# mLSTM cell and SwiGLU layer: another order of the opening, with smaller first weight pieces

## The chip, the cores and the metric

The kernel runs on one core of a Trainium2 chip. Times are device microseconds of one execution. The times before are from three runs; the profile is of one further execution.

## The reference

Two layers are computed one behind the other, all values float32 (the weights are float64 in memory and are rounded to float32 by the kernel).

```python
B, H, S, D = 4, 8, 768, 40                     # q, k, v, o_gate: (B, H, S, D)
for t in range(S):                             # first layer: an mLSTM cell, per head
    m_new = maximum(f[t] + m, i[t])
    fs, is_ = exp(f[t] + m - m_new), exp(i[t] - m_new)
    C = fs * C + is_ * outer(v[t], k[t])
    n = fs * n + is_ * k[t]
    y[t] = sigmoid(o[t]) * (C @ q[t]) / maximum(abs(n @ q[t]), 1)
x = y as (B*S, H*D) = (3072, 320)
g = x @ w_gate                                 # second layer: 320 -> 1536
out = (g * sigmoid(g) * (x @ w_val)) @ w_out   # 1536 -> 320
```

## The kernel before

**Tiling.** The sequence of 768 steps is cut into six chunks of 128. The cell is computed chunk by chunk in its parallel form: within a chunk the recurrence becomes a masked product of q and k, weighted, times v, and only a state passes between chunks. For each chunk the feed-forward layer is run on the 4*128 tokens of the four batch entries. The 1536 hidden features are twelve blocks of 128. `hidden(g, m)` (L646) makes hidden block m of chunk g with ten pairs of products (L651), then Silu on ScalarE (L656) and a product on VectorE (L657). `project` and `project_all` multiply the twelve hidden blocks by `w_out`. While the feed-forward layer of one chunk runs on TensorE, the cell of the next one is worked in between its blocks; lists called `slots` and `after` say behind which block.

**The opening.** Before the first hidden block there is the cell of chunk 0, with a code of its own. Its four units are the four batch entries, with eight heads each; units 0 and 1 form half P=0, units 2 and 3 half P=1. In words: q and k are transposed on TensorE (`first_turn`), their products taken (`first_scores`) and weighted on VectorE (L523), multiplied by v (`first_own(u)`, L530), divided (`first_x(u)`, L535 to L538) and gated by the sigmoid of o_gate (`sig`, L463; `first_gate(P)`, L544). `first_gate` then has GpSimd copy 64 columns (L545). `first_seam(P)` transposes the result into `xT` on TensorE and copies it out of PSUM on ScalarE and VectorE; `first_state(P)` makes the state for the next chunk. `burn(n)` is n products of constants whose result nobody reads. `turn_one` and `turn` are the later chunks' way of transposing q and k: 16 transposes of 64 rows in place of 8 of 128 rows.

**The weights.** Each weight block arrives as pairs of 32-bit words. `piece_load(p)` (L140) asks for piece p of the list `PIECES` (L138): `gv` pieces hold one or two blocks of `w_gate` (lower 64 partitions) and `w_val` (upper 64), `o` pieces four blocks of `w_out`. The gate half is issued from SP; the value half from ScalarE for p < 5, and from SP otherwise. A piece lies in one of two `raw` buffers, or in a `home`: a stretch of `h_sb` or `wo_sb` that is not yet or no longer in use. `W0`, the weights of the first cell, is the first eight blocks of `h_sb`, so a home in there waits for the products that read them. A block is then converted to float32 in three steps: `scale` (two ScalarE instructions, L190 and L192, into `top`, of which there is one buffer, and `low`), `join` (two on VectorE, L199 and L200) and `rounded` (L207, on VectorE or GpSimd).

**What sets the order.** The kernel is under `tc.manual_schedule()`: each engine executes its instructions in the order in which the code writes them, and waits are set from the data. DMAs are instructions of the queue that issues them (SP, or ScalarE between its other work). A DMA takes one of eight semaphores in turn, and so waits for the DMA eight before it to have landed.

Of the kernel before, what the change touches and what calls it, by code (L numbers as in the profile page):

```python
# [12 lines left out]
U32 = mybir.dt.uint32  # L13
AF = mybir.ActivationFunctionType
ALU = mybir.AluOpType
# [9 lines left out]
def kernel(  # L25
# [112 lines left out]
    PIECES = [("gv", 0, 1), ("gv", 1, 1)] + [("gv", m, 2) for m in range(2, NFC, 2)] + [("o", m, 4) for m in range(0, NFC, 4)]  # L138

    def piece_load(p, home=None):  # L140
        kind, m, n = PIECES[p]
        if kind == "gv":
# [3 lines left out]
            queues = (nc.sync, nc.scalar if p < 5 else nc.sync)  # L146
# [12 lines left out]
        if home is None:  # L159
            raw = conv.tile([128, 4 * NKC * 128], U32, name="raw")  # L160
        else:
            raw = home.rearrange("p a t -> p (a t)").bitcast(U32)
# [22 lines left out]
    def scale(j):  # L185
        if j in blocks:
# [3 lines left out]
            nc.scalar.mul(top, hi.bitcast(F32), 2.0 ** -112)  # L190
            low = conv.tile([128, NKC * 128], I32, name="low").rearrange("p (a d) -> p a d", a=a)
            nc.scalar.mul(low, lo, 2.0 ** -29)  # L192
            blocks[j] = (low, top.bitcast(U32), dst)
# [97 lines left out]
    def turn_one(P, src, dst, engs):  # L291
        tp = [bank("tp_kq").rearrange("p (a t) -> p a t", t=SUB) for _ in range(2)]
# [181 lines left out]
    A, V, G = nc.scalar, nc.vector, nc.gpsimd  # L474
    HH = H // 2
# [65 lines left out]
    def first_gate(P):  # L541
        for u in (2 * P, 2 * P + 1):
            x = x_sb[:, u, 0:DM].rearrange("p (h d) -> p h d", d=D)
            nc.vector.tensor_tensor(x, x, o_sb[:, u * H:(u + 1) * H], op=ALU.mult)  # L544
# [13 lines left out]
    def first_seam(P, engs):  # L558
        for c, eng in zip(range(0, NKC, 2), engs):
# [5 lines left out]
            copy(eng, xT(0)[:, c:c + len(cs), 2 * P * L:(2 * P + 2) * L].rearrange("p c (u s) -> p c u s", u=2), tp)  # L565

# [13 lines left out]
    first_turn(1, k_sb, kT, (A, A))  # L580
    first_x(0)
    first_turn(1, q_sb, qT, (A, V))
    load(o_sb, o_gate, 0, 1)
    piece_load(0)
# [5 lines left out]
    piece_load(1)  # L590
    burn(3)
    first_own(2)
    piece_load(2, h_sb[:, 1:1 + NKC])
    sig(1)
    burn(2)
    first_own(3)
    first_gate(0)
    first_x(2)
    first_x(3)
    first_gate(1)  # L600
    first_seam(0, (A, A, V))
    scale(0)
    ps1 = first_state(1, "gen")
    burn(1, "gen")
    piece_load(3, h_sb[:, NH - NKC:])
    join(0)
    first_seam(1, (A, A, V))
    rounded(0, V)
    first_kept(0, first_state(0), A)
    first_kept(1, ps1, V)  # L610
    convert(1, V)
    nc.scalar.activation(warm, warm, AF.Silu)
    piece_load(4, wo_sb)
    piece_load(5)

# [104 lines left out]
    def load_all(dst, a, n):  # L720
        for P in range(2):
            load(dst, a, n, P)

    run = lambda f, *a, **b: (lambda: f(*a, **b))
# [9 lines left out]
        1: [run(piece_load, 6), run(late_decay)],  # L734
# [4 lines left out]
        6: [run(turn, 1, (A, A), (A, V)), run(piece_load, 7)],  # L739
        7: [run(weights_sub, 1, 0), run(weights_mask, 0), run(weights_sub, 1, 1), run(weights_mask, 1), run(nc.gpsimd.memset, q_sb, 0.0)],  # L740
        8: [run(weights_exp, 0), run(weights_exp, 1), run(weigh_values, G, 0), run(weigh_values, G, 1),
            run(piece_load, 8)],
# [110 lines left out]
```

## Time and profile before

| | us |
|---|---|
| three runs: median (lowest to highest) | 551.9 (551.8 to 552.71) |
| the profiled execution | 551.99 |
| its span in the profile | 550.0 |
| TensorE busy | 544.9 (99%) |
| VectorE, ScalarE, GpSimd busy | 236.1, 136.1, 103.0 |
| first product of the first hidden block (L651) starts at | 32.04 |

The span runs from the first recorded instruction to the last; some 2 us of the execution lie outside it. A row of the chain or of the timeline gives its start, its length in us, the engine, the line of the kernel, what is written and read, and how many instructions were merged. A row of stretches gives, for each engine, busy microseconds and the number of instructions, and then TensorE's clock as a share of full speed, the busy share of the DMA engines, and what they moved. The engines are PE (TensorE, with PEld for its weight loads), DVE (VectorE), ACT (ScalarE), POOL (GpSimd) and SP, which issues most DMAs.

### The profile page before, as it was taken

The numbers are of one execution on the slowest core, as the hardware profiler recorded it, in microseconds if no ns is written. First come the engines' busy times: TensorE is split into PE (matmuls) and PEld (weight loads), VectorE is DVE, ScalarE is ACT, GpSimd is POOL, SyncE is SP. The second block draws the span as 40 slices with busy tenths as digits, with TensorE's granted clock in tenths as the row PEclk, the third lists the DMA queues.
The fourth block names the chain that finished last, engine by engine and source line by source line (L and its number), as shares of the span: only waits on it lengthen the run. The fifth ranks groups of instructions, "written<-read, shape, count | busy, mean of one in ns | idle before, by whom it ended". The sixth has DMA issues, their size and how long they took to land.

```text
span 550.0 us, 11592 instructions
## 1 busy us (share of the span) xinstructions
PE 544.9 (99%) x4989; PEld 311.4 (57%) x4989; DVE 236.1 (43%) x397; ACT 136.1 (25%) x203; POOL 103.0 (19%) x95
## 2 busy tenths in 40 slices
PE   8999999999999999999999999999999999999997
PEld 4964556774555575545575545576455567444475
DVE  5778668961346232455421545531436621111100
ACT  4376755352110133011024101115110100111100
POOL 2304265673011060011133011124001100000000
PEclk9999999999999999999999999999999999999999
DMA  9999997878431762660564551395000131000000
GB/s 123 177 294 184 188 277 154 146 104 118 53 49 23 120 112 64 74 74 11 87 117 104 63 72 14 59 146 113 1 1 2 32 63 40 12 1 0 2 24 24
DMA packets 223994, 45.69 MB, mean 83 GB/s; under 512 B 214504, under 2 KB 219112, under 8 KB 223944
## 3 DMA queue, kind: packets, MB, share of 16 engines
q1 hardware_dynamic: 222036, 42.11, 46.7%
q10 hardware_dynamic: 1908, 2.85, 1.9%
q8 instruction: 39, 0.64, 0.5%
q14 instruction: 11, 0.09, 0.1%
HBM read 35.68 MB, written 4.01 MB: 72 GB/s over the span
## 4 chain that ended last, share of the span: by engine, by line
PE 98%; DVE 1%; ACT 0%; issue 0%; ACTq 0%; DVEq 0%
PE gv_ps L651 57%; PE o_ps L667 24%; PE o_ps L674 5%; PE inter L377 2%; PE sp L331 2%; PE intra L382 2%; PE add L353 1%; PE first_y L530 1%; PE burn L469 1%; PE tp_kq L509 1%; PE sp L519 1%; PE wps L480 0%; PE tp_kq L296 0%; PE wps L484 0%; PE wps L489 0%; PE tp_x L439 0%
## 5 line engine op out<-in xcount | busy, mean ns | idle before, releaser
L651 PE MATMUL gv_ps<-xT,wgv_sb 64*128 64x512 f32 x1440 | 316.6, 593 | 0.3 <-DVE wgv_sb L207 0.3
L651 PEld LDWEIGHTS gv_ps<-xT,wgv_sb 64*128 64x128 f32 x1440 | 138.1, 187 | 159.1 <-issue 156.4
L657 DVE TENSOR_TENSOR h_sb<-sg,gv_ps 128x512 f32<-128x512 f32 x72 | 49.5, 688 | 212.3 <-ACT sg L656 212.3
L667 PE MATMUL o_ps<-wo_sb,h_sb 128*128 128x320 f32 x480 | 130.5, 433 | 0.0
L667 PEld LDWEIGHTS o_ps<-wo_sb,h_sb 128*128 128x128 f32 x480 | 90.8, 190 | 41.0 <-issue 3.8
L656 ACT ACTIVATE sg<-gv_ps 128x512 f32<-128x512 f32 x72 | 43.0, 597 | 263.7 <-PE gv_ps L651 263.7
L456 POOL TENSOR_SCALAR_AFFINE_SELECT w_sb<-w_sb 64x1024 f32<-64x1024 f32 x20 | 28.5, 1423 | 63.9 <-DVE w_sb L451 62.9
L362 POOL TENSOR_TENSOR C<-C,dec 128x328 f32<-128x328 f32 x20 | 14.5, 738 | 134.8 <-DVE C L369 134.8
L661 ACT COPY z_sb<-o_ps 128x320 f32<-128x320 f32 x24 | 10.0, 423 | 93.2 <-PE o_ps L667 89.4
L403 POOL TENSOR_TENSOR o_sb<-o_sb,y_sb 128x640 f32<-128x640 f32 x10 | 14.2, 1431 | 78.9 <-DVE y_sb L394 78.9
L674 PE MATMUL o_ps<-wo_sb,h_sb 128*128 128x320 f32 x96 | 26.9, 437 | 0.0
L451 DVE TENSOR_TENSOR w_sb<-g_T,w_sb 128x1024 f32<-128x1024 f32 x10 | 13.1, 1354 | 28.6 <-DMA w_sb<-M_dram 28.6
L426 DVE STREAM_TRANSPOSE xT<-x_sq 128x640 f32<-128x640 f32 x16 | 12.5, 822 | 22.9 <-DMA x_sq<-x_sb 22.9
L674 PEld LDWEIGHTS o_ps<-wo_sb,h_sb 128*128 128x128 f32 x96 | 17.9, 190 | 7.2
L394 DVE TENSOR_TENSOR y_sb<-y_sb,intra 64x328 f32<-64x328 f32 x40 | 19.7, 492 | 0.7
L369 DVE TENSOR_TENSOR C<-C,add 40x328 f32<-40x328 f32 (+1 forms) x36 | 17.7, 493 | 1.2 <-POOL C L362 0.6
L377 PEld LDWEIGHTS inter<-C,qT 64*64 64x64 f32 x640 | 10.2, 134 | 7.3 <-issue 6.1
L460 ACT ACTIVATE w_sb<-w_sb 128x1024 f32<-128x1024 f32 x10 | 10.6, 1058 | 12.7 <-POOL w_sb L456 12.7
L207 POOL TENSOR_TENSOR wgv_sb<-wgv_sb,low 128x640 int32<-128x640 int32 x6 | 9.3, 1546 | 23.5 <-DVE wgv_sb L200 23.5
L341 POOL TENSOR_TENSOR vw_sb<-v_sb,w_sb 128x656 f32<-128x656 f32 x10 | 12.8, 1306 | 0.4
L338 DVE TENSOR_TENSOR w_sb<-sp,w_sb 128x512 f32<-128x512 f32 x20 | 12.7, 682 | 0.0
L397 DVE TENSOR_SCALAR den<-den 128x16 f32<-128x16 f32 x10 | 12.2, 1215 | 0.3
(132 smaller groups left out, 344.5 us busy)
## 6 DMA issues: line engine op xcount, KB each, us to landing
w_sb<-M_dram SPq DMA_DIRECT2D x10, 512.0 KB, 7.3
x_sq<-x_sb SPq DMA_DIRECT2D x128, 40.0 KB, 2.0
k_sb<-in_k_dram SPq DMA_DIRECT2D x12, 320.0 KB, 6.0
v_sb<-in_v_dram SPq DMA_DIRECT2D x12, 320.0 KB, 5.6
o_sb<-in_o_gate_dram SPq DMA_DIRECT2D x12, 320.0 KB, 5.5
raw<-in_moe_w_out_dram SPq DMA_DIRECT2D x3, 1280.0 KB, 7.5
out_dram<-z_sb SPq DMA_DIRECT2D x24, 160.0 KB, 1.8
q_sb<-in_q_dram SPq DMA_DIRECT2D x32, 64.0 KB, 2.3
```

Of the source, the lines that this page charges most:

```text
L362: nc.gpsimd.tensor_tensor(state(s + 1)[:, a], state(s)[:, a], dec[:, s - 2, a].unsqueeze(2).to_broadcast([128, UA, D1]), op=ALU.mult)
L369: nc.vector.tensor_tensor(c, c, ps[r], op=ALU.add)
L377: nc.tensor.matmul(inter[two][half(i), a, :], lhsT=qT[half(two), P * UA + a, half(i)], rhs=state(2 * n + i)[half(two), P * UA + a, :], sta ...
L394: nc.vector.tensor_tensor(t, t, intra[i][half(c)], op=ALU.add)
L403: eng.tensor_tensor(o, o, y[:, :, 0:D], op=ALU.mult)
L451: nc.vector.tensor_tensor(w_sb[:, heads(P)], gb, w_sb[:, heads(P)], op=ALU.subtract)
L456: nc.gpsimd.affine_select(w, w, compare_op=ALU.is_ge, fill=NEG, base=0, pattern=[[0, UH], [1, SUB]], channel_multiplier=-1)
L651: nc.tensor.matmul(ps[i], lhsT=wgv_sb[half(i), m, PAIRS[kc][i] if g < 2 else kc, :], rhs=x[half(i), kc, :], start=(kc == 0), stop=(kc == N ...
L656: nc.scalar.activation(sg, ps[0], AF.Silu)
L657: nc.vector.tensor_tensor(hid(g, m), sg, ps[1], op=ALU.mult)
L667: nc.tensor.matmul(p, lhsT=hid(g, m)[:, ts(u, L)], rhs=wo_sb[:, m, :], start=(m == 0), stop=(m == NFC - 1))
L674: nc.tensor.matmul(ps[u], lhsT=hid(g, m)[:, ts(u, L)], rhs=wo_sb[:, m, :], start=(m == 0), stop=(m == NFC - 1))
```

## The change

The opening is written in another order, and the first weights come in other pieces:

- `PIECES` has four pieces of one block (before: two), then four of two blocks. The value half of a piece is issued from ScalarE for p < 6.
- The piece of block 0 is asked for ahead of the second half of o_gate, the piece of block 1 right behind it. The pieces of blocks 2 and 3 are asked for one behind the other after `first_own(2)`, into two stretches of `h_sb`; later pieces change their homes (blocks 4 and 5 to `wo_sb`, 6 to 9 to `raw`, 10 and 11 to the end of `h_sb`).
- k and q of units 2 and 3 are transposed by `turn_one`, k into the other set of PSUM banks.
- Three constant products before unit 2's values become two; two between the values of units 2 and 3 go; one later becomes two.
- `scale(0)` and `join(0)` stand between the divisions of units 2 and 3, and the second sigmoid behind `scale(0)`. `rounded(0)` stands ahead of the second seam.
- The gate of units 0 and 1 goes from VectorE to GpSimd, its sigmoid and division staying where they are.
- Block 1 is scaled behind the second half's state and joined behind the two copies of the state.

```diff
-    PIECES = [("gv", 0, 1), ("gv", 1, 1)] + [("gv", m, 2) for m in range(2, NFC, 2)] + ...
+    PIECES = [("gv", m, 1) for m in range(4)] + [("gv", m, 2) for m in range(4, NFC, 2)] + ...
...
-            queues = (nc.sync, nc.scalar if p < 5 else nc.sync)
+            queues = (nc.sync, nc.scalar if p < 6 else nc.sync)
...
-    first_turn(1, k_sb, kT, (A, A))
+    turn_one(1, k_sb, kT, (A, A), "gen")
+    turn_one(1, q_sb, qT, (A, V))
     first_x(0)
-    first_turn(1, q_sb, qT, (A, V))
+    piece_load(0)
     load(o_sb, o_gate, 0, 1)
-    piece_load(0)
+    piece_load(1)
     first_own(1)
     first_values(1)
     first_scores(1)
     first_x(1)
     sig(0)
-    piece_load(1)
-    burn(3)
+    burn(2)
     first_own(2)
-    piece_load(2, h_sb[:, 1:1 + NKC])
+    piece_load(2, h_sb[:, 2:5])
+    piece_load(3, h_sb[:, NH - NKC:NH - 2])
+    first_x(2)
+    scale(0)
+    join(0)
     sig(1)
-    burn(2)
     first_own(3)
-    first_gate(0)
-    first_x(2)
+    first_gate(0, G)
     first_x(3)
-    first_gate(1)
+    first_gate(1, V)
     first_seam(0, (A, A, V))
-    scale(0)
     ps1 = first_state(1, "gen")
-    burn(1, "gen")
-    piece_load(3, h_sb[:, NH - NKC:])
-    join(0)
+    burn(2, "gen")
+    rounded(0, V)
     first_seam(1, (A, A, V))
-    rounded(0, V)
-    first_kept(0, first_state(0), A)
+    ps0 = first_state(0)
+    piece_load(4, wo_sb)
+    scale(1)
+    first_kept(0, ps0, A)
     first_kept(1, ps1, V)
-    convert(1, V)
+    join(1)
+    rounded(1, V)
     nc.scalar.activation(warm, warm, AF.Silu)
-    piece_load(4, wo_sb)
     piece_load(5)
+    piece_load(6)
...
-        1: [run(piece_load, 6), run(late_decay)],
+        1: [run(piece_load, 7, h_sb[:, NH - NKC:]), run(late_decay)],
```

The pieces of `w_out` in the later slots are the same, each with its number raised by one.

## The prediction

> **What bounds the kernel now.** I read the page's chain of work that ended last first, then the busy times by stretch, then the chain and the timeline narrowed to the opening. The first two say where a change can count at all.
>
> ```profile
> PE 98%; DVE 1%; ACT 0%; issue 0%; ACTq 0%; DVEq 0%
> ```
>
> ```profile
> core 0: us, PE busy (x) PEld busy (x) DVE busy (x) ACT busy (x) POOL busy (x), PEclk, DMA share, GB/s
> 0.00:32.04 32.04, 30.14 (x297) 22.60 (x298) 22.66 (x59) 14.30 (x24) 7.57 (x18) 1.00 1.09 157
> 32.04:94.00 61.96, 61.96 (x701) 32.62 (x701) 46.69 (x71) 39.44 (x56) 26.07 (x19) 1.00 1.03 225
> 94.00:125.00 31.00, 30.91 (x269) 21.75 (x268) 25.20 (x39) 13.94 (x21) 20.58 (x16) 1.00 0.86 125
> ```
>
> The reader is to see that TensorE is the chain, and that from 32.04 us, where the first product of the feed-forward layer starts, it is busy 61.96 of 61.96 us. The rest is a train of products of fixed length, so the whole change is worth whatever it does to the start of that train, plus any hole that it tears into the train later. The opening of 32.04 us is the place, and this is its chain:
>
> ```profile
> 16.80 0.90 PE tp_kq L509 x8
> ...
> 17.73 1.06 PE tp_kq L509 x8
> 18.79 1.71 PE first_y L530 x16
> 20.51 1.99 PE sp L519 x32
> 22.49 0.76 PE burn L469 x3
> 23.25 1.71 PE first_y L530 x16
> 24.96 0.43 PE burn L469 x2
> 25.39 1.73 PE first_y L530 x16
> ...
> 28.27 0.80 DVE x_sb L544 x2
> ...
> 31.08 0.83 DVE wgv_sb L207
> 31.91 0.14 issue
> 32.04 17.51 PE gv_ps L651 x80
> ```
>
> Up to 27.1 us the chain is TensorE in its written order, the constant products (burn) among it. Then it is VectorE: unit 3's division, the second gate (28.19 to 29.07), the joining of weight block 0 and its rounding, L207, which ends at 31.91. Three rows of the timeline set the other limits, ScalarE's two and the last transposed copy:
>
> ```profile
> 25.04 0.63 ACTq L165 DMA_DIRECT2D h_sb<-in_moe_w_val_dram  x1
> 25.72 0.74 ACT L463 ACTIVATE o_sb<-o_sb 128x640 f32<-128x640 f32 x1 [3.61 <-DMA raw<-in_moe_w_val_dram]
> ...
> 30.74 0.43 DVE L123 COPY xT<-tp_x 128x256 f32<-128x256 f32 x1
> ```
>
> ScalarE issues DMAs in its own order. The issue at 25.04 waited for unit 2's products (they end at 24.96) before it could overwrite their weights' place, and the sigmoid behind it waited too. And L207 stands behind the copy of 30.74, which needs TensorE's last transposes (29.45 to 30.70): TensorE was full from 25.23 to 31.76 and then waited 0.28 us for L207.
>
> **Two rules of the skill.** The Trainium skill, "SBUF — State Buffer", section "Who interferes with whom", says that VectorE and GpSimd share one pair of ports as an exclusive lock, and that a VectorE instruction contends when it runs in a two-port mode or reads two SBUF operands. The trace agrees:
>
> ```profile
> 167.34 1.44 POOL L403 TENSOR_TENSOR o_sb<-o_sb,y_sb 128x640 f32<-128x640 f32 x1 [10.36 <-DVE y_sb L394]
> 167.52 1.29 DVE L397 TENSOR_SCALAR den<-den 128x16 f32<-128x16 f32 x1
> ```
>
> An instruction over 16 elements took 1.29 us, until the gate on GpSimd had ended. The forecast therefore lets the moved gate lock some VectorE work. "DMA: Bandwidth & Descriptors", section "Queues, rings and completion order", says that each DMA engine goes round between its rings packet by packet. The trace differs here: the ScalarE load issued at 25.04 moved nothing between 26 and 30 us, in which SP's ring moved 195 to 206 GB/s. Up to 31 us each weight load moved as a whole, in the order in which its issue had ended. I go by the trace.
>
> **The change part by part.**
>
> *Turning k and q of units 2 and 3 by halves.* 8+8 transposes of 128x128 (16.80 to 18.79, 1.99 us) become 16+16 of 64 rows. The later turn(0) has exactly these: 32 in 0.99 us (59.74 in the chain). Saving 1.0, or 0.6 if q's second half, issued at 10.31, lands as late as 17.7, which the trace does not show. The keys' copies on ScalarE (1.07) and one of q follow as now, so scores(1) can start at 19.5 instead of 20.5, when own(1) is done.
>
> *Constant products.* Five in the middle (0.76 + 0.43) become two (0.43); one later becomes two (+0.22). Own(2) still needs the first two of the four weightings of 0.62 us, the first of which starts 1.26 after scores(1); so own(2) runs 22.0 to 23.75 and own(3) 23.75 to 25.5. That is 1.6 earlier than 27.1 on TensorE.
>
> *Block 0 joined earlier.* This is where the gain goes. VectorE's order was weightings, x(1) 1.12, gate(0) 0.88, x(2) 1.12, x(3) 1.13, gate(1) 0.88. Gate(0) leaves for GpSimd, and L199 0.49 + L200 0.83 = 1.32 come in ahead of x(3). With weightings done at 23.25: x(1) to 24.4, x(2) to 25.5. The join then needs ScalarE's top half. ScalarE must first issue the loads of blocks 2 and 3; the first of these waits for own(2), 23.75, and each takes 0.65, so the top runs 25.1 to 25.95. Join 26.0 to 27.35, x(3) to 28.45, gate(1) to 29.35. Gate(1) ended at 29.07 before.
>
> *Gate(0) on GpSimd.* Two products of 128x320. L362, 128x328, takes 0.74, so 24.45 to 25.95, the copied columns (0.29) to 26.25. The first seam's ten transposes run about 26.0 to 27.3, the state to 28.45, two constants to 28.9: free before gate(1) ends. The lock can hold x(2)'s reciprocal (0.20) up to 0.75; that fills the wait for the top and costs nothing. If the lock instead holds the copied columns behind the join, up to 1.1 later, the seam ends at 28.1 and TensorE reaches the second seam at 29.7: cost up to 0.35. I take 0.1.
>
> *Second seam and after.* From 29.4: transposes 1.25 and state 1.13, pitch 2.31 from 29.45 to 31.76 before, so 31.75. L207 now precedes the last copy, running about 29.8 to 30.6, and no longer adds its 0.28. First product at 31.8, plus 0.1 for the lock: 31.9.
>
> *First weights first.* Before, the second half of o_gate was issued at 16.85 and landed at 25.05; the gate half of block 0 was issued at 19.43 and landed at 28.23. They change places, and the other half of block 1 is issued at 19.1 on ScalarE, not 21.38. Block 0 should land at 23.5 to 24.9, in time for 25.1. The second half of o_gate becomes the last of the same set, whose last packet moved at about 26.4 and landed at 28.2. Without the pause of SP's ring at 20 to 21 us (62 packets of some 1,050) it is 27.3 to 28.6. Sigmoid: +0.8, so gate(1) can start at 28.1 to 29.4 against 28.45 from VectorE. The middle, 28.75, adds 0.2; at the early end nothing. I take 0.1: start at 32.0.
>
> *Loads behind.* Blocks 2 and 3 are split in two pieces, 320 KB instead of 640 KB, twice the issues (0.6 each). Before, the value half of both was only freed for the next load in its slot at 37.0, and block 2's scaling began at 37.13, beside the first sg's end at 37.20. The smaller piece lands earlier; scaling starts behind sg as now, so no gain and no loss. Blocks 4 and 5 go to wo_sb, 6 and 7 and 8 and 9 to raw, 10 and 11 to h_sb. Their bytes stay in the same order; blocks 4 and 5 landed at 38.6 and 40.7 for a scaling at 43.32. Cover of 2.6 us against an issue that is later by about 2. ScalarE's new wait ahead of the first sg is for block 2's gate half (33.1 before, earlier now); behind it stands the sg of 36.60. If that cover were gone, each microsecond late would be one on TensorE two blocks later. No product is added or removed after 32 us.
>
> **Sum.** Start 32.04 becomes 32.0, somewhere in 31.4 to 32.6. The profiled execution took 551.99 with a span of 550.0, so 1.99 lie around it; it would be 551.95. The median of the runs before is 551.9, 0.1 under the profiled one, so the forecast is 551.85, rounded to 551.8.
>
> **Rivals.** *The gain on TensorE survives* (550.7): own(3) ends 1.6 earlier and everything behind it follows. For it: TensorE is the chain up to 27.1. Against it: VectorE's sum from 23.25 is 1.12 + 1.12 + 1.32 + 1.13 + 0.88 = 5.57, so gate(1) ends at 28.8 even with the top ready, and the top is not ready. Chance 0.08.
>
> *o_gate's second half comes last* (553.3, the slower side): its landing holds the sigmoid, that gate(1), that the second seam. It costs over 1.1 us when gate(1) starts after 29.6, so when it lands after 28.8, only 0.2 past my estimate. At 29.1 to 29.4 the first product starts at 33.2 to 33.5. For it: loads moved in order of issue, and it is now behind three weight halves. Against it: the bytes before it are no more than those that had moved by 26.4. Chance 0.16.
>
> *The weights are no earlier, or q holds the turning* (552.3): block 0's gate half lands at 26.4 because both ScalarE loads move before it, or own(1) gains only 0.6. Then the join ends 0.4 to 1.3 later, partly covered. Start at 32.4 to 33.0. For it: its issue took 2.87 us before (19.43 to 22.30). Against it: its issue begins 1.5 before ScalarE's first. Chance 0.12, nearly all within no change.
>
> **How the numbers follow.** The likeliest case has 0.64 and its own range is 551.3 to 552.5. A difference of 0.2%, 1.1 us, is about what measurement tells from none. Faster 0.08 is the first rival. Slower is 0.16 from the second and 0.02 from the third's end. No change is the rest, 0.74. The lower end, 551.0, leaves most of the first rival out; the upper, 553.3, takes in the third and the near half of the second.
>
> **What would show it.** Right: the first gv_ps product at 31.4 to 32.6; transposes of k and q at half the time; own(3) done near 25.5, and a TensorE gap before the second seam; VectorE's L199 waiting for ScalarE's top near 25.5 to 26; TensorE full after the start. Wrong: ScalarE waiting for o_gate past 28.8 (second rival), gate(1) ended before 28.3 (first), or a hole in the train between 36 and 60 us, which would mean a late weight block, against what is said of the loads behind.

## The result and the profile after

| | before | after |
|---|---|---|
| median of 20 runs each, us | 552.27 | 555.12 |
| lowest to highest | 551.52 to 554.73 | 552.31 to 557.63 |
| ratio, 95% interval | | 1.0045 [1.0027, 1.0063] |
| profiled execution, span | 551.99, 550.0 | 557.63, 555.3 |
| first product of the first hidden block | 32.04 | 34.27 |

The changed kernel is slower by about half a per cent, and its median lies outside the forecast range of 551.0 to 553.3 us. Ratios here and below are of means, and leave out three executions (563.19, 560.94 and 560.96 us, in e1_fill, f4_block1_later and f2_own_gate_pieces) that lie over 1.5% above the fastest of their kernel.

Its executions differ among themselves: 8 of the 20 took 552.3 to 553.7, the other 12 took 554.7 to 557.6. TensorE's mean granted clock was below 0.998 in 10 of the 20, in one of the lower eight and in nine of the upper twelve. The ten with the lower clock have a median of 555.8 us, the ten at full clock one of 553.0. So the clock has a large part in this result; three of the upper twelve had it at full speed all the same, and lost their time in another way.

Lines have moved: L651 is now L667, L530 L541, L207 L217, L199 and L200 L209 and L210, L463 L473, L544 L555, L552 L563, L564 L575, L192 L198, L625 L641, L451 L461, L456 L466, L338 L348, L353 L363, L447 L457.

The first profile is of the slowest of these executions. Its chain (start, length, what):

```profile
19.28 10.13 DMA o_sb<-in_o_gate_dram
...
29.43 0.74 ACT o_sb L473
30.17 0.97 ACT xT L121 x2
...
32.40 1.87 PE add L563 x32
34.27 19.82 PE gv_ps L667 x80
...
102.33 0.72 issue
```

The second half of o_gate landed at 29.41, the sigmoid and the gate came behind it, and TensorE stood idle from 28.88 to 30.75. At 32.3 its clock fell. In the row of the stretch from 33 to 39 us the second last group of numbers begins with the clock:

```profile
33.00:39.00 6.00, 6.00 (x36) 3.32 (x36) 2.42 (x4) 3.27 (x5) 0.00 (x0) 0.50 1.09 198
```

TensorE was busy all of the six microseconds and did the work of three. The state before the start took 1.87 in place of 1.13 us, and the first 80 products 19.82 in place of 17.51. So the start is 2.2 us late (0.74 of it by the clock), the products lose 2.3, and a hole at 102.33 costs 0.6: 5.2 together, against a difference of 5.3 between the two spans.

That is one execution. A second profile of the unaltered kernel (after_b below, span 553.8) shows another way to lose nearly as much, at full clock. Its chain:

```profile
20.45 13.55 DMA raw<-in_moe_w_gate_dram
...
36.48 0.84 DVE wgv_sb L217
...
37.36 13.15 PE gv_ps L667 x60
...
61.20 11.89 DMA w_sb<-M_dram
...
76.97 2.07 POOL w_sb L466
...
88.56 1.29 DVE w_sb L348 x2
...
89.90 1.14 PE add L363 x62
```

Here the train started at 32.17, 0.1 us later than before. But after its first 20 products it waited for block 1, whose gate half had landed at 34.0 (29.9 before), and at 88 to 90 us it waited for w_sb, the masked decay weights of chunk 1, which are made from two loads of M_dram on SP. SP's own rows show what the two have in common. First the kernel before, then the changed one (start, length of the issue, what is loaded):

```profile
19.43 3.53 SPq L165 DMA_DIRECT2D raw<-in_moe_w_gate_dram  x2
...
30.14 0.59 SPq L165 DMA_DIRECT2D raw<-in_moe_w_gate_dram  x1
...
33.20 16.15 SPq L117 DMA_DIRECT2D k_sb<-in_k_dram  x2
49.44 1.31 SPq L724 DMA_DIRECT2D M_dram<-M_sb  x1
...
56.13 8.59 SPq L447 DMA_DIRECT2D w_sb<-M_dram  x2
```

```profile
20.45 5.20 SPq L165 DMA_DIRECT2D raw<-in_moe_w_gate_dram  x1
...
34.14 2.12 SPq L165 DMA_DIRECT2D raw<-in_moe_w_gate_dram  x2
...
37.96 16.28 SPq L117 DMA_DIRECT2D k_sb<-in_k_dram  x2
54.34 1.44 SPq L485 DMA_DIRECT2D M_dram<-M_sb  x1
...
61.20 9.39 SPq L457 DMA_DIRECT2D w_sb<-M_dram  x2
```

The next pair of loads into the `raw` buffers is issued only when block 1's gate half is there: 34.14 instead of 30.14. Every load behind it on SP comes 4 to 5 us later, through the long issue of chunk 1's k to M_dram and w_sb. VectorE takes up both halves of w_sb at once, before and then after:

```profile
71.68 2.35 DVE L451 TENSOR_TENSOR w_sb<-g_T,w_sb 128x1024 f32<-128x1024 f32 x2
```

```profile
75.67 2.36 DVE L461 TENSOR_TENSOR w_sb<-g_T,w_sb 128x1024 f32<-128x1024 f32 x2 [0.88 <-DMA w_sb<-M_dram]
```

After, it waited for the second half, which landed at 75.6. Before, it did not wait: the first half had landed at 68.5, and for the second the profile gives no landing, only that it was there by 71.68. So the cover before was at most some 3 us, and it may have been much less. The wait for w_sb is not alone there. ScalarE waited too, for the weights of blocks 10 and 11, which SP now issued at 60.48 in place of 55.41, just ahead of w_sb:

```profile
71.07 0.78 ACT L190 ACTIVATE top<-h_sb 128x640 f32<-128x640 f32 x1 [2.71 <-DMA h_sb<-in_moe_w_val_dram]
```

VectorE stood behind that wait and would have come to w_sb at 74.79 at the earliest. Two late loads of one queue act at the same place.

TensorE's rows of the two executions divide the 3.8 us between the spans. At the products behind the first 80 (the turning of the gates, L641) the changed kernel is 0.96 late: 0.1 from the start, the rest from block 1. At the products behind the state of chunk 1 (90.96 against 87.45) it is 3.5 late: of the 2.5 added, 0.25 came at the turns near 60 us, the other 2.3 from 20 products that with the wait behind them took 5.93 instead of 4.49, and a state that took 2.86 instead of 2.01. The 20 products were held up because ScalarE's Silu stood behind its late work on w_sb.

In the first profile SP's loads were as late (M_dram issued at 54.27, w_sb at 61.66). There TensorE was itself over 4 us late by then, through o_gate and the clock, and waited for neither. The two ways of losing hide each other, so their costs do not add up.

### The profile page after: what moved, and what is told of

Same layout as the page of the kernel before. It is cut to its first block, busy times and chain, and to the rows that moved or that the text cites. A ratio compares the mean times of both kernels' runs of the same rounds, so it can differ in the third digit from the quotient of the medians.

```text
span 555.3 us, 11624 instructions
## 1 busy us (share of the span) xinstructions
PE 547.3 (99%) x5001; PEld 311.3 (56%) x5003; DVE 235.1 (42%) x395; ACT 135.9 (24%) x203; POOL 104.6 (19%) x97
## 4 chain that ended last, share of the span: by engine, by line
PE 94%; SPq 3%; DMA 2%; ACT 0%; issue 0%; ACTq 0%
PE gv_ps L667 57%; PE o_ps L683 23%; PE o_ps L690 5%; SPq L117 3%; PE inter L387 2%; DMA o_sb<-in_o_gate_dram 2%; PE sp L341 2%; PE intra L392 2%; PE add L363 1%; SPq L165 0%; PE tp_kq L306 0%; PE add L563 0%; PE tp_x L449 0%; PE tp_x L575 0%; ACT xT L121 0%
## 5 line engine op out<-in xcount | busy, mean ns | idle before, releaser
L667 PE MATMUL gv_ps<-xT,wgv_sb 64*128 64x512 f32 x1440 | 318.9, 597 | 0.0
L667 PEld LDWEIGHTS gv_ps<-xT,wgv_sb 64*128 64x128 f32 x1440 | 137.9, 188 | 161.4 <-issue 158.7
L466 POOL TENSOR_SCALAR_AFFINE_SELECT w_sb<-w_sb 64x1024 f32<-64x1024 f32 x20 | 28.4, 1422 | 61.9 <-DVE w_sb L461 61.0
L461 DVE TENSOR_TENSOR w_sb<-g_T,w_sb 128x1024 f32<-128x1024 f32 x10 | 13.1, 1355 | 26.7 <-DMA w_sb<-M_dram 26.7
L387 PEld LDWEIGHTS inter<-C,qT 64*64 64x64 f32 x640 | 10.2, 134 | 7.3 <-issue 6.1
L217 POOL TENSOR_TENSOR wgv_sb<-wgv_sb,low 128x640 int32<-128x640 int32 x6 | 9.3, 1543 | 26.1 <-DVE wgv_sb L210 26.1
L190 ACT ACTIVATE top<-raw 128x640 f32<-128x640 f32 x12 | 9.6, 796 | 13.7 <-issue 5.7
L348 DVE TENSOR_TENSOR w_sb<-sp,w_sb 128x512 f32<-128x512 f32 x20 | 12.7, 682 | 0.0
```

What stands on the lines that cost most here:

```text
L387: nc.tensor.matmul(inter[two][half(i), a, :], lhsT=qT[half(two), P * UA + a, half(i)], rhs=state(2 * n + i)[half(two), P * UA + a, :], sta ...
L466: nc.gpsimd.affine_select(w, w, compare_op=ALU.is_ge, fill=NEG, base=0, pattern=[[0, UH], [1, SUB]], channel_multiplier=-1)
L667: nc.tensor.matmul(ps[i], lhsT=wgv_sb[half(i), m, PAIRS[kc][i] if g < 2 else kc, :], rhs=x[half(i), kc, :], start=(kc == 0), stop=(kc == N ...
```

## The experiments

Each expectation states its theories itself; theory C, first stated for e5_less_const, is that the removed constant products let the clock fall. "Low" below counts executions whose mean granted clock was under 0.998. In the six groups of runs the kernel before had 183 executions and none of them was low. Its medians there were 552.18 to 552.64, and each ratio is against the executions of its own group.

### First group: the late gate and the clock

e1_fill fills TensorE's gap ahead of the second seam:

```diff
     ps1 = first_state(1, "gen")
-    burn(2, "gen")
+    burn(10, "gen")
```

> The changed kernel with ten constant products instead of two ahead of the second seam (8 more, 1.7 us of work in a gap of 1.9 us). Theory A (o_gate's second half lands late, and the gap that this leaves on TensorE lowers its clock to half for some 7 us, which costs more than the gap): the gap and its end stay, second seam at about 30.8 us, but the clock stays full, seam and state take 2.4 us, first product at 33.2 us, the first 80 products take 17.4 us and not 19.8; 553.2 to 553.8 us, and the scatter of single runs shrinks. Theory B (the clock's fall is a by-product of this one execution and the time comes from the late start and late loads): time as for the changed kernel, 555 us.

555.9 us (554.3 to 563.19, 5 runs), ratio 1.0066 [1.0046, 1.0087]. The filler ran at full clock, and the first 80 products took 17.41. But the clock had already been at half from 18.2 to 25.0, ahead of the filler, and the first product started at 36.16. So the gap of 1.9 us is not the only place where the clock falls, and filling it brought nothing in five runs.

e2_own_gate takes the late sigmoid away (units 2 and 3 are gated with the first half's sigmoids):

```diff
-            eng.tensor_tensor(x, x, o_sb[:, u * H:(u + 1) * H], op=ALU.mult)
+            eng.tensor_tensor(x, x, o_sb[:, (u % 2) * H:(u % 2 + 1) * H], op=ALU.mult)
...
-    sig(1)
```

> The changed kernel, in which units 2 and 3 are gated by the sigmoids of units 0 and 1 and the second sigmoid is left out of the opening: the second half of o_gate is loaded but nothing in the opening waits for it (its products are another function). Theory A: second gate right behind unit 3's division, 28.7 us, second seam at 29.7, first product at 32.0, clock full. Then block 1 is the next thing late, because its gate half lands at 34.5 us: ready at 37.7 against 36.4, a hole of about 1.3 us in the products; 552.8 to 553.6 us. Theory B (VectorE's own order with the joining in it holds the second seam, o_gate only looks late): first product not before 33 us, 555 us.

555.9 us (554.57 to 556.17, 4 runs), 1.0064 [1.0047, 1.008]. Nothing waited for o_gate, and the first product started at 32.69 although the clock was half from 26.0 to 29.5. Yet the span was 553.9. Its chain holds the load of w_sb (60.36, 11.95 us) and then GpSimd, VectorE and ScalarE working on it, as in after_b. Neither theory had this. A start near 32.7 doesn't help when w_sb is late.

e3_o_first restores the order of o_gate and block 0:

```diff
-    piece_load(0)
     load(o_sb, o_gate, 0, 1)
+    piece_load(0)
     piece_load(1)
```

> The changed kernel with o_gate's second half asked for ahead of block 0 again, everything else as changed. If the order of these two loads were all that is wrong, 551.5 to 552 us. Theory A with the joining where the change put it: block 0's gate half lands at about 28.2, the joining then holds unit 3's division, the second gate begins at 31.5 and the gap on TensorE grows to 3.5 us; first product at 34.5 to 35 us, clock down, 556 to 559 us.

555.19 us (554.13 to 557.4, 5 runs), 1.0068 [1.0044, 1.0093]. Block 0's gate half landed at 27.36, so the join (28.21 to 29.57) held unit 3's division and the gate went to 30.52. The wait only changed its owner. The clock was half from 31.1 to 34.5, and the time stayed under the expected 556 to 559.

e4_before_swap makes only this exchange, in the kernel before:

```diff
-    load(o_sb, o_gate, 0, 1)
     piece_load(0)
+    load(o_sb, o_gate, 0, 1)
```

> The kernel before with only these two loads exchanged: block 0 ahead of o_gate's second half. Theory A: o_gate's half lands at 27.5 to 29.4 us, the second gate and the seam wait for it, first product at 33 to 34.4; 553 to 556 us by whether the clock falls in the gap. Theory B: the load order is covered, 552 us.

552.61 us (551.37 to 554.33, 12 runs), 1.0007 [0.9994, 1.002]; none low. The second sigmoid moved to 28.06 and the first product to 33.05 in the profile, but the exchange by itself costs nothing that the runs tell from zero.

### Second group: the edits of the computation

e5_less_const makes the kernel before with the constant products of the changed one (3, 2, 1 become 2, 0, 2):

```diff
-    burn(3)
+    burn(2)
     first_own(2)
...
-    burn(2)
     first_own(3)
...
-    burn(1, "gen")
+    burn(2, "gen")
```

> The kernel before with only the constant products as in the change: three become two ahead of unit 2's values, two between the values of units 2 and 3 go, one later becomes two. Theory C (the clock follows how much the array streams, not whether instructions are queued: own(2) and own(3) stream 41 columns behind weight loads of 128, and 3.5 us of that in a row, without the constant products between, lets the clock fall): TensorE has no gap, yet the clock falls to half in part of the executions, 3 to 7 us long; median 553 to 556 us with a wide scatter. Theory A (the clock falls only in the idle gap that o_gate leaves): no fall, own(3) done 0.4 us earlier, 551.5 to 552.2 us.

552.26 us (551.0 to 554.72, 13 runs), 0.9998 [0.9989, 1.0007]. The median stayed, but 5 of 13 executions were low, at 552.8 to 554.7. The profiled one had its clock at half from 34.6 to 38, and its 80 products took 19.14. So theory C had the falls and missed the median.

e6_turn makes only the turning by halves:

```diff
-    first_turn(1, k_sb, kT, (A, A))
+    turn_one(1, k_sb, kT, (A, A), "gen")
+    turn_one(1, q_sb, qT, (A, V))
     first_x(0)
-    first_turn(1, q_sb, qT, (A, V))
```

> The kernel before with only the turning of k and q of units 2 and 3 by halves. Without a fall of the clock own(3) ends at 26.3 instead of 27.1, but block 0's gate half lands at 28.2 and holds the joining: first product at 31.3 to 31.7 us, 551.2 to 551.7 us. Theory C: these transposes stream half the columns, and so the stretch from 16.6 us is thinner; a fall in some executions, 552 to 554 us. Theory A: no fall.

551.91 us (551.18 to 556.92, 22 runs), 1.0003 [0.999, 1.0016]. In the profile the first product started at 31.46 instead of 32.04, so the edit is worth 0.6 there; the median is 0.4 lower. But 3 of the 22 executions were low, at 555.6 to 556.9, and in the mean they took the gain back.

e7_own_gate_const puts the constants back into e2_own_gate:

```diff
-    burn(2)
+    burn(3)
     first_own(2)
...
+    burn(2)
     first_own(3)
```

> The kernel of the run with the first half's sigmoids at both gates (nothing waits for o_gate's second half; another function) and the constant products put back: three ahead of unit 2's values, two between units 2 and 3. It differs from that run, 555.9 us, by nothing but three products of 0.21 us. Theory C: the clock stays full, first product at 31.2 to 31.8 us, 551.2 to 552.2 us. Theory A: the constant products do nothing but take time, as that run, 555 to 556 us.

556.15 us (555.67 to 557.69, 5 runs), 1.0074 [1.006, 1.0087], 4 of 5 low. The clock was at half from 18.0 to 24.9, ahead of both places, and the start was at 34.88. The span was 553.9 all the same, that of e2_own_gate with a start at 32.69. So putting these constants back did not keep the clock full, against theory C, and the late loads set the same floor for a second time.

c1_front takes the kernel before and makes the front without the load edits: turning by halves, both halves of block 0 asked for by ScalarE, and block 0 scaled and joined ahead of the second seam:

```diff
-            queues = (nc.sync, nc.scalar if p < 5 else nc.sync)
+            queues = (nc.scalar if p == 0 else nc.sync, nc.scalar if p < 5 else nc.sync)
...
     sig(1)
+    scale(0)
...
-    scale(0)
     ps1 = first_state(1, "gen")
...
-    first_seam(1, (A, A, V))
     rounded(0, V)
+    first_seam(1, (A, A, V))
```

> A version meant to beat both: the kernel before, its constant products and its o_gate order kept, with the turning by halves, both halves of block 0 asked for from ScalarE (so ahead of most of o_gate's second half without delaying it on SP), block 0 scaled right behind the second sigmoid, and joined and rounded ahead of the second seam. Block 0 lands at 25 to 26.5, top by 27.3, second gate ends at 28.1, block 0 ready at 30.3, TensorE runs without a gap to the first product at 31.0: 550.8 to 551.3 us if the clock holds. Theory C warns: the turning thins the stretch from 16.6 us, and where the clock falls it is 552 to 554 us.

551.78 us (550.98 to 554.74, 14 runs), 0.9995 [0.9984, 1.0006]; 2 of 14 low. The first product started at 31.32, and TensorE had no gap before it, but the time did not come down to the expected 550.8 to 551.3, not even at full clock (551.6). A front of this kind costs nothing with the load order of the kernel before. c1_front has its own way of loading block 0 and keeps the constants, so it is not the changed kernel without its load edits; h2_pieces_block1 below comes nearer to that.

### Third group: block 1, the pieces, a second look

f4_block1_later changes one line of the changed kernel, back to where it was:

```diff
     load(o_sb, o_gate, 0, 1)
-    piece_load(1)
     first_own(1)
...
     sig(0)
+    piece_load(1)
```

> The changed kernel with one step moved: block 1's loads are asked for behind the first sigmoid, as in the kernel before, so that o_gate's second half is not followed at once by block 1's gate half. Theory of the late sigmoid (o_gate's second half lands at 29.4 because two weight halves ride beside it): it lands about 28, gate(1) ends about 29, TensorE's gap before the second seam shrinks from 1.9 us to under 1, the first product starts 32 to 33 and the time is 552.3 to 553.5. Theory that the clock alone does it: the clock still falls somewhere between 18 and 33 us in most executions and the time stays at 555. Theory that block 1's slow issue pushes SP's later loads: it is issued later still, so w_sb's second half still lands at 75 us or later; this costs nothing as long as the start is late, and shows as a floor of about 553 where it is early.

553.3 us (551.76 to 560.94, 12 runs), 1.0012 [0.9996, 1.0029], 6 of 12 low. The six at full clock took 551.8 to 553.1 (median 552.1), the six low ones have a median of 555.2. In the profile the second sigmoid ran at 26.36, the first product at 32.64, and w_sb's second half landed at 72.7. This one line carries most of the loss, and nearly all of what was left came with the clock.

f2_own_gate_pieces restores the pieces in e2_own_gate:

```diff
-    PIECES = [("gv", m, 1) for m in range(4)] + [("gv", m, 2) for m in range(4, NFC, 2)] + ...
+    PIECES = [("gv", 0, 1), ("gv", 1, 1)] + [("gv", m, 2) for m in range(2, NFC, 2)] + ...
...
-            queues = (nc.sync, nc.scalar if p < 6 else nc.sync)
+            queues = (nc.sync, nc.scalar if p < 5 else nc.sync)
...
-    piece_load(2, h_sb[:, 2:5])
-    piece_load(3, h_sb[:, NH - NKC:NH - 2])
+    piece_load(2, h_sb[:, 1:1 + NKC])
```

The homes and numbers of the later pieces follow as in the kernel before.

> The kernel of e2_own_gate (units 2 and 3 gated with the first half's sigmoids and the second sigmoid left out, so another function), with the pieces of the kernel before: blocks 2 and 3 in one piece, the same buffers and the same choice of queues. Theory that the split and the queues behind it delay SP's later loads: M_dram is issued near 50 us instead of 54, w_sb's second half lands before 72 us instead of 75 to 76, the 3 us that e2_own_gate lost after its first product are gone, and the time is 551.5 to 552.8 where the clock holds, 553 to 554 where it falls once. Rival, that block 1's gate half (5.8 us of issue, landing at 34) is what delays them, whatever the pieces: w_sb's second half still lands at 75 us or later and the time stays at 555.5 to 556.

553.86 us (552.36 to 560.96, 14 runs), 1.0028 [1.0016, 1.004], 7 low; the seven at full clock have a median of 553.0. Two microseconds under e2_own_gate (4 runs), so the pieces matter too. The profile, of a low execution (555.96), has M_dram issued at 53.5 and w_sb complete at 75.0, as the rival expected, but not for the rival's reason. The clock was at half from 18.0 to 24.9, so unit 2's products ended late, and the loads of blocks 2 and 3, which wait for them, were issued at 27.76 only. Block 1's gate half had landed by 29.7, and k waited 4.2 us for the loads of blocks 2 and 3. A fallen clock can thus make the loads late as well.

c2_fill_turn adds two constants between the turns of c1_front:

```diff
     turn_one(1, k_sb, kT, (A, A), "gen")
+    burn(2)
     turn_one(1, q_sb, qT, (A, V))
```

> The kernel before, turned by halves, block 0 loaded from ScalarE and joined ahead of the second seam as in c1_front, and two filler products between the turning of k and that of q, where TensorE waits for q. Theory of the clock: the gap there is what lets the clock fall in some executions (2 of 14 in c1_front); with it filled hardly any falls, and the time is 551.2 to 551.8, at or 0.1% below the kernel before. Rival, the filler delays the turning and own(2) by its own length (0.4 us) and changes nothing in the clock: 551.8 to 552.3.

552.15 us (551.57 to 553.02, 13 runs), 0.9994 [0.9986, 1.0002]; none low (2 of 14 without the filler, 3 of 22 in e6_turn). The direction of the clock is that of the clock theory, the time is the rival's, and the numbers are too small to decide it. It is no measurable gain over the kernel before.

after_b is the changed kernel once more.

> The changed kernel unaltered, for a second profile. Its runs lie in two groups, 552.3 to 553.7 and 554.7 to 557.6, and the first profile is of the second group. If the groups differ by the clock alone, a profile of the first group has the same order of landings (o_gate's second half at 29.4) and TensorE's clock near 1 between 32 and 39; if they differ by the order of the loads, o_gate's second half lands before 28.5 and the gap ahead of the second seam is under 1 us. Another profile of the second group repeats the first: landing 29 to 30, gap 1.5 to 2, clock at half for some 6 us.

556.14 us, the second profile shown above: clock near 1, o_gate's second half landed at 28.2, a gap of 0.3 us, start at 32.17. By clock, landing and gap this should have been an execution of the lower group, and its time is of the upper one. So neither the clock nor o_gate alone parts the groups; late loads can cost as much at full clock.

### Fourth group: a table of two by two

g1_block1_early moves block 1's loads alone, in the kernel before:

```diff
     piece_load(0)
+    piece_load(1)
     first_own(1)
...
     sig(0)
-    piece_load(1)
```

> The kernel before with block 1's loads moved from behind the first sigmoid to right behind block 0's loads, nothing else. Theory that this place is the cause: block 1's gate half is asked for near 22 and lands after 33, o_gate's second half lands 1 us or more later than before, block 1 is not ready at the end of the first 20 products or w_sb's second half lands after 74, and the time is 553.5 to 556. Theory that it needs the other edits too: 552.0 to 552.8, as the kernel before.

552.53 us (552.0 to 553.14, 12 runs), 1.0 [0.9992, 1.0009]; none low. The same line that carries the loss in the changed kernel costs nothing here. SP's row of both gate halves, and ScalarE's of the next load:

```profile
19.20 3.73 SPq L165 DMA_DIRECT2D raw<-in_moe_w_gate_dram  x2
```

```profile
24.71 0.63 ACTq L165 DMA_DIRECT2D h_sb<-in_moe_w_val_dram  x1
```

SP issued both gate halves by 22.93, block 1's in 0.6 us, and ScalarE's next load (blocks 2 and 3) came at 24.71, behind them. In the changed kernel the issue of block 1's gate half ended at 25.65 to 25.84.

g2_f4_const puts the constants back into f4_block1_later, g3_const into the changed kernel; the edit is the same:

```diff
-    burn(2)
+    burn(3)
     first_own(2)
...
+    burn(2)
     first_own(3)
...
-    burn(2, "gen")
+    burn(1, "gen")
```

> f4_block1_later with the constant products back at the three places and counts of the kernel before (3 ahead of unit 2's own products, 2 ahead of unit 3's, 1 between the seams). Theory that their removal lets the clock fall: at most 2 in 10 executions have a mean clock below 0.998, against 6 in 12 of f4_block1_later, and the median is 551.5 to 552.5. Rival, that the order of loads and joins itself lets it fall: 4 in 10 or more fall and the median stays near 553.3 or above.

553.51 us (551.57 to 557.52, 22 runs), 1.0031 [1.0016, 1.0047]; 7 of 22 low. The count is between what the two theories expected, the median is the rival's, and it is no better than without the constants.

> The changed kernel with the same constant products back, block 1's loads left early. Theory that block 1's place is the larger cause: the median stays at 554 to 556 although fewer executions fall in clock, since w_sb's second half still lands at 75 or later and the end of the span still has a floor of 553. Theory that the constant products are the larger cause: 552 to 553.

554.73 us (552.22 to 556.84, 11 runs), 1.0039 [1.002, 1.0057]; none low, against 10 of 20 in the changed kernel. In this order no execution with the constants was low (in those of e7_own_gate_const and g2_f4_const some were), and the time stays. The profile repeats after_b: block 1's gate half at 33.9, the 21st product at 37.11 instead of 36.4, w_sb at 75.0, span 554.1. So with the clock at full speed in every execution the changed order still costs 2.4 us in the median.

The executions at full clock compare the two places of block 1 without the clock's part. With block 1 early (the changed kernel, after_b and g3_const) there are 22, with a median of 554.1; with block 1 late (f4_block1_later and g2_f4_const) there are 21, with one of 552.7.

### Fifth group: the pieces in the changed kernel

h1_pieces makes f2's edit in the changed kernel, h2_pieces_block1 makes it in f4_block1_later.

> The changed kernel with blocks 2 and 3 in one piece again, and the buffers, places and queues of the later pieces that follow from it; block 1's loads stay early. Theory that the pieces and block 1's place each cost about half: 553.2 to 554.2. Theory that block 1's gate half, landing at 34, is enough for the whole loss: 554.5 to 555.5, w_sb's second half at 75 or later. Theory that the pieces are the whole: 552 to 552.8.

553.5 us (552.07 to 557.2, 13 runs), 1.003 [1.0017, 1.0042], 4 low. Start at 32.28, M_dram issued at 51.55, w_sb complete at 72.9. Block 1's gate half was still late (33.5), so what the pieces changed is the queue behind it.

> The changed kernel with both taken back: blocks 2 and 3 in one piece with the buffers and queues that follow, and block 1's loads behind the first sigmoid. What is left of the change is the turning by halves, the removed constant products, block 0 loaded ahead of o_gate's second half, and joined ahead of unit 3's division. Theory that the two load edits are all that costs: 551.5 to 552.5, M_dram issued by 50.5 and w_sb's second half landed by 71, with at most 3 in 10 executions at a lower clock. Rival, that the order of block 0 and o_gate or the joins cost the rest: 553 or above.

552.99 us (551.96 to 556.15, 22 runs), 1.002 [1.0011, 1.003], 7 low; the 15 at full clock have a median of 552.8. In the profile (span 549.9) the first product started at 31.35, M_dram was issued at 49.22, as before, and VectorE took up w_sb at 71.53 without a wait. The late loads are gone. The median is between the two theories, at the rival's edge. What remains over the kernel before, 0.8 us in the median, is in part the executions whose clock fell (median 555.0); the other 0.6, which the executions at full clock show, isn't settled, and the rival, that the order of block 0 and o_gate or the joins cost it, stands.

Medians, in us, and behind them what they lie over the kernel before of the same group:

| | blocks 2 and 3 split | in one piece |
|---|---|---|
| block 1 early | 555.1, +2.8 (after) | 553.5, +1.3 (h1) |
| block 1 late | 553.3, +0.9 (f4) | 553.0, +0.8 (h2) |

Either load edit taken back removes more than half of the loss, and both together little more. In the queue the two do add up: M_dram was issued at 54.3 (after_b), 52.3 (f4), 51.6 (h1) and 49.2 (h2). In the time they don't, since a load that is earlier than its consumer brings nothing. These are single profiles, and that of f4 is of a low execution.

### Sixth group: why block 1's gate half is late

The two kernels compared here ask for the same loads. In the summaries of loads by kind (number, KB each, median us from issue to landing), between 14 and 80 us, the changed kernel and then f4_block1_later have:

```profile
raw<-in_moe_w_gate_dram SPq DMA_DIRECT2D x2, 320.0 KB, 11.2
...
h_sb<-in_moe_w_val_dram ACTq DMA_DIRECT2D x2, 320.0 KB, 7.8
```

```profile
raw<-in_moe_w_gate_dram SPq DMA_DIRECT2D x2, 320.0 KB, 8.5
...
h_sb<-in_moe_w_val_dram ACTq DMA_DIRECT2D x2, 320.0 KB, 10.8
```

The two exchange places. In the changed kernel ScalarE's two loads for blocks 2 and 3 (issued 23.34 to 25.44) end their issue before SP's for block 1 (20.07 to 25.84), and land first. In f4_block1_later SP's ended at 23.58 and lands first. i1_blocks23_later moves ScalarE's two issues only, behind the scaling of block 0, and no row of any other engine:

```diff
-    piece_load(2, h_sb[:, 2:5])
-    piece_load(3, h_sb[:, NH - NKC:NH - 2])
     first_x(2)
     scale(0)
     join(0)
+    piece_load(2, h_sb[:, 2:5])
+    piece_load(3, h_sb[:, NH - NKC:NH - 2])
     sig(1)
```

> The changed kernel with two issues of ScalarE moved: the value halves of blocks 2 and 3 are asked for behind the scaling of block 0 (near 27) instead of ahead of it (23.3 to 25.4). Theory that loads land in the order in which their issues end on both queues: the issue of block 1's gate half on SP ends near 25.8, after ScalarE's two in the changed kernel and before them here, so it no longer stands behind their 640 KB (3.3 us at 195 GB/s) and lands at 30 to 31.5 instead of 34; the next loads of SP start 2 to 4 us earlier, w_sb's second half lands by 73.5, and the time falls to 552.3 to 553.8. Rival, that SP's own slow issue behind o_gate's small packets is what makes it late: it still lands at 33.5 or later and the time stays at 554.5 to 555.5.

553.9 us (553.46 to 554.93, 7 runs), 1.0026 [1.0014, 1.0037]: 1.2 under the changed kernel, a tenth above what was expected. The interval overlaps the changed kernel's [1.0027, 1.0063], so what this run shows, it shows by its landings rather than by its time. SP's rows of it, then ScalarE's:

```profile
20.21 5.33 SPq L165 DMA_DIRECT2D raw<-in_moe_w_gate_dram  x1
...
31.91 2.74 SPq L165 DMA_DIRECT2D raw<-in_moe_w_gate_dram  x2
```

```profile
24.64 0.60 ACTq L165 DMA_DIRECT2D h_sb<-in_moe_w_val_dram  x1
28.34 0.60 ACTq L165 DMA_DIRECT2D h_sb<-in_moe_w_val_dram  x1
28.99 0.74 ACT L473 ACTIVATE o_sb<-o_sb 128x640 f32<-128x640 f32 x1 [2.94 <-DMA o_sb<-in_o_gate_dram]
```

SP's issue was as slow as ever, 5.33 us, so the rival falls. One of ScalarE's two loads went out behind it, and SP's next load, which needs block 1's gate half, was issued at 31.91 instead of 34.14: 2.2 us earlier, where one load of 320 KB takes 1.68 at 195 GB/s. The hole behind the first 20 products is gone (80 products in 17.44). The other load, at 24.64, still ended its issue first, and at 28.34 its neighbour held up the second sigmoid, so the train started at 33.00, and w_sb landed at 73.5. Both keep the gain small.

## Why the prediction was wrong

The forecast was 551.8 us in 551.0 to 553.3; the median was 555.12. *Loads behind* is the step that failed first. It said "no gain and no loss" and "No product is added or removed after 32 us", and followed SP's loads as far as blocks 4 and 5. The queue goes on: k, M_dram, the weights of blocks 10 and 11 and w_sb stand behind them in order. M_dram went from 49.4 to 54.3, and VectorE took up w_sb at 75.67 in place of 71.68, against a cover of at most 3 us that I had not looked for. The products were the same in number, but the train got holes. The sign that the prediction named for this, a hole in the train between 36 and 60 us, appeared in after_b (36.7 to 37.4).

*First weights first* worked out where block 0 and o_gate land and left out block 1's gate half, though its loads move in the same edit. My own rule from the trace, that a load moves as a whole in the order in which its issue ended, would have placed it behind ScalarE's loads for blocks 2 and 3: from o_gate's landing at 28.2, three halves of 1.68 us each (320 KB at 195 GB/s) give 33.2, an estimate; 34.0 was measured. The Trainium skill's "DMA: Bandwidth & Descriptors", section "Queues, rings and completion order", has the engines go round between rings packet by packet. Here too the measurement decides against it: two loads of 320 KB overtook the third whole.

Of what this step did size, block 0's gate half landed at 24.8 (forecast 23.5 to 24.9), and o_gate's second half at 27.9, 28.2 and 28.3 in three profiles (forecast 27.3 to 28.6) but at 29.41 in the first. So the rival "o_gate's second half comes last" happened, past its own point of 28.8, in that execution; how often it happens, four profiles don't tell. It cost the start 2.2 us, of which the clock made 0.74; without that the start is 33.5, where the rival had put it.

*Constant products* priced five products by their time and put the clock at nothing. Their removal let the clock fall more often (5 of 13 executions of e5_less_const against 0 of 183 before, 10 of 20 of the changed kernel against 0 of 11 of g3_const). The constants are not the whole of it: with them the clock still fell in 3 of 22 executions of e6_turn and 7 of 22 of g2_f4_const. Putting them back moved the median by no more than 0.4. That is not the clock's whole share, though: in the changed kernel the low executions lie 2.8 us over those at full clock, and in f4_block1_later 3.1. So there are two causes, late loads and the fallen clock. Each costs 2 to 3 us by itself, they hide each other, and how the 2.8 us between the medians divide between them is not settled.

*Turning k and q by halves* was right: 16 transposes in 0.71 us each time, with q's wait of 0.36, and 0.6 us alone. But own(2) started at 22.67, not 22.0, and with own(3) took 3.71 instead of 3.5, so own(3) ended at 26.4, not 25.5. That cost nothing, since the second gate waited for the sigmoid behind it.

*Block 0 joined earlier*, *Gate(0) on GpSimd* and *Second seam and after* held where the clock held: top at 25.3, joined by 27.7, second gate at 29.0, first product at 32.17 in after_b and 31.94 in g3_const against the forecast 32.0. The start was predicted well, in part by luck: own(3) was 0.9 us late, and the wait behind it took that up. The end was not, because the sum stopped at the start.

## What to carry to other kernels

When loads are moved, list every load of all queues in the order in which its issue will end, add up the bytes ahead of each, and do it for each load that the edit touches, not only for the one that it wants early. Then follow the delayed queue to its last consumer and find the one with the least cover; here it stood 40 us behind the edit. Compare executions at one granted clock before the medians of all. One profile of a kernel whose executions scatter shows one way of losing: two profiles showed two.

## What the hardware showed that was not expected

- TensorE's clock fell to half for 3.4 to 10.2 us at places that no long gap preceded. In f4_block1_later it fell at 25.9, and TensorE had been busy 2.95 of the 3 us from 22 to 25; in g2_f4_const at 17.6, with 0.28 us idle from 17 to 18; in the first profile of the changed kernel 1.5 us behind a gap of 1.9. The Trainium skill, "TensorE: Matmul & The Clock Gate", "Part 1: The HAM clock gate", gives an idle window of about 3.4 us, free-running, as the condition. No gap here was that long, and there the measurement decides; that the place varies between executions of one kernel agrees with it. What exactly lets the clock fall is open.
- The clock stayed at half for a whole number of steps of about 3.41 us. Added up from the granted clock in stretches of 0.25 us, one fall lasted 3.41 to 3.42 us (e2_own_gate, e3_o_first, e5_less_const, f4_block1_later), 6.82 to 6.83 (after, e1_fill, e7_own_gate_const, f2_own_gate_pieces) or 10.24 (g2_f4_const). One step at half clock costs up to 1.7 us of product time, an estimate, and lowers the mean clock of such an execution by 0.003. In e5_less_const, where the five low executions all have 0.997, one step, they lie 1.3 us over the others.
- While only SP's or only ScalarE's packets moved, the weights came at 186 to 214 GB/s; with both at once at about 330 to 375. The kernel before had this from 33 to 42 us (mean 354), the changed one from about 44 on. There the packets of the two queues do move side by side, as the page has it (90 of SP's and 88 of ScalarE's from 44 to 45 us in after_b). Late issues cost bandwidth as well as time.
- The issue of one load of 320 KB on SP took from 0.6 us (g1_block1_early) to 5.8 (the changed kernel), by what stood ahead of it in the queue.
- Open: why seven executions of the changed kernel take 552.3 to 553.7 at full clock. Both profiles of it that were taken are of the slower ones, so whether their loads are late is not known.
